# High halves of the second product by ScalarE, earlier writes of plain weight quarters, raw tokens in token buffers

## The chip, the core and the metric

The kernel runs as one program on one core of a Trainium2 chip. The metric is the device time of one execution in microseconds. TensorE does the matmuls (PE in the profile; PEld is its weight load), VectorE is DVE, ScalarE ACT, GpSimd POOL, and SyncE (SP) issues the transfers.

## The reference

Windowed attention over 8 batches, 8 heads, 576 positions and head size 64, and then a feed-forward layer over the 4608 tokens of 512 numbers:

```python
mask_plain = (rel >= 0) & (rel < window)                                    # window 32, heads 0 to 3
mask_dil = (rel >= 0) & (rel < window * dilation) & (rel % dilation == 0)   # dilation 4, heads 4 to 7
attn = softmax(where(mask, q @ k.T / 8, -1e9)) @ v      # (8, 8, 576, 64), then (4608, 512)
h = x @ w_in                                            # (4608, 2048)
g = h * clip(h + 3, 0, 6) / 6
out = g @ w_out                                         # (4608, 512)
```

## The kernel before

**Precision.** Every operand x of a large matmul is held as a high half (a cast to fp32r) and a low half (x minus the high half), and a product is three matmuls: high by high, low by high, high by low.

**Tokens** go in blocks (chunks) of CH = 384. Blocks 0 to 3 are multiplied plainly: first() makes the 12 matmuls of `gemm1` for one of 16 slices f of the hidden layer (L529 to L531), the gate, its high half (L544) and its low half (L548), and second() makes the 9 matmuls of `gemm2` (L579 to L581). Blocks 4 to 11 form four groups g of two blocks, and each 2 by 2 product of blocks is made with seven products in place of eight (Strassen and Winograd's scheme): A11, A12, S2, S1, S3, A22, S4.

**First product of a group** (`first_product`, `multiply`, L732 to L734): for each of eight pairs k of slices seven products of six matmuls; the token operands, `cell(i)`, are filled by `fill` (L700 combines raw tokens on VectorE, L703 casts the high half on ScalarE, L707 subtracts the low half on VectorE). The gate of a result is L982 (ScalarE) and L987 (VectorE). **Second product** (`second_products`): 56 halves, for each a high half gh (L1173), a low half gl (L1179) and six matmuls (L723), with sums of gated tiles between (L1144, VectorE). Its results are taken from the banks by ScalarE (L1096, L1125) and VectorE (L1111). HIGH_BY names the engine of each gh: all "p", GpSimd.

**Weights.** `combine` makes sums of the weights' quarters (words L624, sums L632, high L636, low L641) and `combo_out` (L659) writes them to two tensors in HBM, sums and rights. `combo_plain` (L650) writes the plain quarters there, 24 transfers of 256 KB for each side, after a slice pair's last use in blocks 0 to 3. `load_sums` (L673) brings the tiles back, 512 KB each, into a ring of eight.

**Attention** goes through 48 trios. After the first twelve, `attend` issues a block of scores and values (L213, L231), the exponentials, the turning of tiles, and a load of kq (L184) and v (L193) for the trio two further on. In `low` GpSimd subtracts low halves (L436) for blocks 0 to 3, or copies the tokens of blocks 4 to 11 to raw tiles (L438), from the pool wpool (36 slots, tag w). xh and xl hold the high and low halves of three blocks.

**Order.** ORDER, written by hand, sets the instructions of about the first 75 us. From there each operation is entered with `op(engine, us, do, after, lag, takes, gives, ahead)`: a cost, what it waits for, the buffers that it takes and gives, and how far ahead of its due time it may go. `_in_time` then walks all engines in time and picks, on each, what can start first, and among those what is due first. TensorE's order is fixed; the others' follow from the costs. SyncE's transfers are entered as its issue time with a fixed lag until they land. Every engine runs its queue in order.

Of the kernel before, what the change touches and what calls it, by code (L numbers as in the profile page):

```python
# [19 lines left out]
P = 128  # L20
QB = 32
DIL = 4
# [16 lines left out]
SLACK = 0.4  # L39
SPOTS = (35, 1), (38, 1), (41, 1), (44, 1), (47, 1), (50, 1), (53, 1), (56, 1)  # L40
LEAD_SUMS = 300.0
# [42 lines left out]
def windowed_attention_ffn(ctx: ExitStack, tc: tile.TileContext, qk, vp, w, mask, out, out_t):  # L84
# [87 lines left out]
    def w_tile(name, shape, dtype=F32):  # L172
        return wpool.tile([P, *shape], dtype, name=name, tag="w")
# [211 lines left out]
    def raw_of(block, kind):  # L385

        if (block, kind) not in raws:
            raws[block, kind] = w_tile("raw", [2, CH])
        return raws[block, kind]

    def spans(t):

        b, kind, part = trios[t]
        half = CH // 2
        at = half * part
        while at < half * (part + 1):
            c, i0 = divmod(at, CLS) if kind else (0, at)
            n = min((CLS if kind else S) - i0, half * (part + 1) - at)
            token = b * S + (DIL * i0 if kind else i0)
            if b >= 2:  # L400
                room = CH - token % CH
                n = min(n, room // DIL if kind else room)
            yield at - half * part, n, c, i0, token
            at += n

    def pieces_of(t):

        b, kind, part = trios[t]
        xu = xfs[t].rearrange("p (u f) -> p u f", u=2)
        found = []  # L410
        for at, n, c, i, token in spans(t):
            src, plain = xu[:, :, at : at + n], token < PLAIN * CH
            if plain:
                whole = lambda x: x[:, 2 * kind : 2 * kind + 2, b % 2 * S : b % 2 * S + S]
            else:
                whole = lambda x, token=token: raw_of(token // CH - PLAIN, kind)
                i = token % CH // (DIL if kind else 1)
# [102 lines left out]
    def gemm1(n):  # L520
        c, f = steps[n]
        assert 2 * f in converted and all(x in written for x in trios if c in chunks(*x))
        read[c] += 1
        r0 = (c * CH) % (2 * S)
        ph = ps_h.tile([P, CH], F32, name="ps_h")
        for kt in range(NK):
            a, b = xh[:, kt, r0 : r0 + CH], xl[:, kt, r0 : r0 + CH]
# [3 lines left out]
            ins = nc.tensor.matmul(ph, lhsT=wt(f, 1)[:, ks], rhs=a, start=False, stop=(kt == NK - 1))  # L531
        phs[n] = ph
        return ins
# [140 lines left out]

    seventh = []

    def cell(i):

        if i == S3:
            if not seventh:  # L680
                seventh.extend(w_tile(name, [2, CH], F32R) for name in ("x7h", "x7l"))
            return seventh
        block, k = {A11: (1, 0), A12: (1, 1), S2: (2, 0), S1: (2, 1), A22: (0, 0), S4: (0, 1)}[i]
        return [x[:, 2 * k : 2 * k + 2, block * CH : (block + 1) * CH] for x in (xh, xl)]

# [16 lines left out]
    def fill_high(g, i):  # L702
        nc.scalar.copy(cell(i)[0], source(g, i))  # L703

    def fill_low(g, i):
        hi, lo = cell(i)
        nc.vector.tensor_tensor(out=lo, in0=source(g, i), in1=hi.bitcast(F32), op=ALU.subtract)  # L707
# [18 lines left out]

    def multiply(at, k, i, bank, start):

        tile_, (h, l) = ring[at][:, rows_at(place[k, i] // 2).index(row(k, i))], cell(i)
        for kt in range(2):  # L730
            ks = slice(kt * P, (kt + 1) * P)
            nc.tensor.matmul(bank, lhsT=tile_[:, 0, ks], rhs=h[:, kt], start=(start and kt == 0), stop=False, skip_group_check=True)  # L732
            nc.tensor.matmul(bank, lhsT=tile_[:, 0, ks], rhs=l[:, kt], start=False, stop=False, skip_group_check=True)  # L733
            nc.tensor.matmul(bank, lhsT=tile_[:, 1, ks], rhs=h[:, kt], start=False, stop=(kt == 1), skip_group_check=True)  # L734
# [60 lines left out]
    def attend(bs, pools):  # L795
# [20 lines left out]
        for ts in scores:  # L816
# [15 lines left out]
            if ts + NLOAD < T:  # L832
                landed_k[ts + NLOAD] = op("SP", 0.4, lambda ts=ts: load_qk(ts + NLOAD), [beat], lag=5.0, ahead=EVER)
        for tv in values:
# [11 lines left out]
            if tv + NLOAD < T:  # L846
                landed_v[tv + NLOAD] = op("SP", 0.4, lambda tv=tv: load_v(tv + NLOAD), [beat], lag=5.0, ahead=EVER)
            pieces = [(n, token // CH) for _, n, _, _, token in spans(tv)]
            touched = {c for n, c in pieces if c >= PLAIN} - {c for c, kind in raw_seen if kind == trios[tv][1]}
            raw_seen.update((c, trios[tv][1]) for c in touched)  # L850
# [7 lines left out]
    def put_out(c, tt, bank, r, after, parts, last):  # L858
# [16 lines left out]
        freed.append(done_[-1])  # L875
        op("SP", 0.45, lambda: nc.sync.dma_start(out=out[r : r + P, :], in_=o[0]), done_, lag=2.5, gives=SLOT if last else ())

# [4 lines left out]
    def combine(side, k):  # L882
        x = op("DVE", 0.69, lambda: combo_words(side, k, 0, nc.vector), takes=[("w", 2, 1)], ahead=LEAD_SUMS)
# [46 lines left out]
    def bring(at):  # L930
        if at < 2 * GROUPS * STREAM:
# [3 lines left out]
            elif at < 2 * STREAM:  # L935
                sources = [(1, RIGHT_TURNS[2 * (i - STREAM) + j][1]) for j in range(2)]
            ring_landed[at] = op(
                "SP", 0.5, lambda: load_sums(at), [*(x for y in sources for x in combined[y]), ring_used.get(at - RING)],
                lag=6.0, takes=[("w", 1, 3)], ahead=14.0,
            )  # L940
# [13 lines left out]
    def fill(g, free_after):  # L954
# [42 lines left out]
    def first_product(g, k, i, at_bank, name, after=()):  # L997
# [3 lines left out]
        def do():  # L1001
            if start:
                at_bank[name] = ps_a.tile([P, DM], F32, name="ps_x", tag="ps_a")
            multiply(at, k, i, at_bank[name][:, :CH], start)

# [5 lines left out]
        ring_step(at, x)  # L1011
        used[i] = x
        return x

# [70 lines left out]
    def second_products(g):  # L1085
# [46 lines left out]
        def ship(name, after):  # L1132
# [4 lines left out]

            op("SP", 0.45, do, after, lag=2.5, gives=SLOT)

# [379 lines left out]
```

## Time and profile before

| what | us |
|---|---|
| three runs | 866.81, 871.83 (median), 874.95 |
| the profiled execution | 866.8 |
| its span, first to last instruction | 865.0 |
| TensorE, weight loads busy | 837.4, 774.1 |
| VectorE, ScalarE, GpSimd busy | 699.1, 477.8, 225.6 |
| mean granted clock | 0.992 |
| transfers | 214.71 MB, 248 GB/s on average |

Matmuls are pipelined: one of 384 columns lasts about 335 ns, and the next starts about half of that later. So the sum of durations is no measure of TensorE's work; distances between starts are. The groups of matmuls by stage: `gemm1` and `gemm2` with the attention of the first trios up to about 330 us, then first and second products of the four groups in turn. The second products lie at about 415 to 488, 549 to 618, 678 to 746 and 799 to 861 us.

### The profile page before, as it was taken

What the parts mean: (1) busy time and instruction counts of PE and PEld (TensorE: products, weight loads), DVE (VectorE), ACT (ScalarE), POOL (GpSimd) and SP (SyncE); (2) the same over time, 40 slices, a digit from 0 to 9 for tenths busy, and PEclk for the clock granted to TensorE, in tenths of its full rate; (3) what the DMA queues carried; (4) which work ended last, traced back from release to release, by engine and by line L of the source; (5) the groups of instructions that cost most, each with busy time, mean ns of one, the idle gap of its engine ahead of it and who ended that gap; (6) DMA issues with size and microseconds to landing.
All of it is one profiled execution on the core that took longest, in us unless ns stands there. A gap on an engine that the chain in (4) does not pass through costs nothing.

```text
span 865.0 us, 22224 instructions
## 1 busy us (share of the span) xinstructions
PE 837.4 (97%) x8758; PEld 774.1 (89%) x8758; DVE 699.1 (81%) x1307; ACT 477.8 (55%) x1170; POOL 225.6 (26%) x338
## 2 busy tenths in 40 slices
PE   7899999999999999988999999999999999999998
PEld 4698898988888898977888999998999998999998
DVE  4899986567767988966999977999876899545995
ACT  3788675235999875876801599501598401354100
POOL 0000000010132220000858001558001458001574
PEclk8999999999999999998999999999999999999999
DMA  8856435235338799999974998974988773996371
GB/s 293 278 168 198 125 120 170 86 134 167 127 124 298 254 351 386 380 392 394 366 248 152 315 333 305 339 260 155 328 301 311 266 246 140 356 378 219 131 279 56
DMA packets 115768, 214.71 MB, mean 248 GB/s; under 512 B 7504, under 2 KB 40272, under 8 KB 115664
## 3 DMA queue, kind: packets, MB, share of 16 engines
q1 hardware_dynamic: 115664, 213.29, 71.2%
q8 instruction: 69, 1.13, 0.5%
q14 instruction: 35, 0.29, 0.1%
HBM read 174.47 MB, written 38.80 MB: 247 GB/s over the span
## 4 chain that ended last, share of the span: by engine, by line
PE 78%; DVE 10%; issue 5%; DMA 4%; ACT 2%; POOL 1%; SPq 0%; DVEq 0%; POOLq 0%
PE ps_o L723 15%; PE ps_x L732 8%; PE ps_x L733 8%; PE ps_x L734 8%; DVE gl L1179 6%; PE ps_h L529 5%; PE ps_h L530 5%; PE ps_h L531 5%; PE ps_o L579 5%; PE ps_o L581 5%; PE ps_o L580 5%; DVE g L1144 2%; DMA v<-in_v 2%; PE ps_b L231 2%; PE ps_a L213 1%
## 5 line engine op out<-in xcount | busy, mean ns | idle before, releaser
L723 PE MATMUL ps_o<-gh,ring 128*128 128x384 f32 x896 | 231.9, 335 | 0.1
L1173 POOL CAST gh<-g 128x384 fp32r<-128x384 f32 x224 | 170.5, 793 | 131.8 <-DVE g L987 61.4
L723 PEld LDWEIGHTS ps_o<-gh,ring 128*128 128x128 f32 x896 | 162.4, 188 | 0.8 <-POOL gh L1173 0.4
L723 PE MATMUL ps_o<-gl,ring 128*128 128x384 f32 x448 | 154.2, 344 | 5.8 <-DVE gl L1179 4.7
L1179 DVE TENSOR_TENSOR gl<-g,gh 128x384 fp32r<-128x384 f32 x224 | 152.5, 719 | 1.0 <-POOL gh L1173 1.0
L732 PE MATMUL ps_x<-xh,ring 128*128 128x384 f32 x384 | 132.3, 345 | 2.7 <-DMA ring<-sums 2.7
L733 PE MATMUL ps_x<-xl,ring 128*128 128x384 f32 x384 | 129.9, 338 | 0.0
L734 PE MATMUL ps_x<-xh,ring 128*128 128x384 f32 x384 | 129.6, 338 | 0.0
L723 PEld LDWEIGHTS ps_o<-gl,ring 128*128 128x128 f32 x448 | 84.0, 188 | 17.8 <-DVE gl L1179 17.1
L544 POOL CAST gh<-t 128x384 fp32r<-128x384 f32 x36 | 23.5, 654 | 276.1 <-DVE t L540 276.1
L529 PE MATMUL ps_h<-xh,wi 128*128 128x384 f32 x256 | 87.8, 343 | 0.0
L531 PE MATMUL ps_h<-xh,wi 128*128 128x384 f32 x256 | 86.1, 336 | 0.0
L530 PE MATMUL ps_h<-xl,wi 128*128 128x384 f32 x256 | 86.1, 336 | 0.0
L438 POOL COPY raw<-xf 128x96 f32<-128x96 f32 (+2 forms) x65 | 27.6, 493 | 206.2 <-ACT xf L377 164.2
L1096 ACT ACTIVATE o<-ps_o 128x384 f32<-128x384 f32 x32 | 15.7, 492 | 114.5 <-PE ps_o L723 105.9
L732 PEld LDWEIGHTS ps_x<-xh,ring 128*128 128x128 f32 x384 | 72.6, 189 | 5.9 <-DMA ring<-sums 2.9
L1144 DVE TENSOR_TENSOR g<-g 128x768 f32<-128x768 f32 x64 | 75.2, 1175 | 0.0
L579 PE MATMUL ps_o<-wo,gh 128*128 128x512 f32 x192 | 75.1, 391 | 0.0
L581 PE MATMUL ps_o<-wo,gl 128*128 128x512 f32 x192 | 74.7, 389 | 0.0
L580 PE MATMUL ps_o<-wo,gh 128*128 128x512 f32 x192 | 74.7, 389 | 0.0
L733 PEld LDWEIGHTS ps_x<-xl,ring 128*128 128x128 f32 x384 | 72.6, 189 | 0.2
L734 PEld LDWEIGHTS ps_x<-xh,ring 128*128 128x128 f32 x384 | 72.6, 189 | 0.0
(114 smaller groups left out, 1649.5 us busy)
## 6 DMA issues: line engine op xcount, KB each, us to landing
ring<-sums SPq DMA_DIRECT2D x112, 512.0 KB, 7.5
ring<-rights SPq DMA_DIRECT2D x112, 512.0 KB, 6.4
st<-in_w SPq DMA_DIRECT2D x32, 512.0 KB, 4.2
kq<-in_qk SPq DMA_DIRECT2D x39, 416.0 KB, 4.3
v<-in_v SPq DMA_DIRECT2D x39, 390.0 KB, 5.6
sums<-wi SPq DMA_DIRECT2D x24, 256.0 KB, 6.7
rights<-wo SPq DMA_DIRECT2D x24, 256.0 KB, 6.6
out<-o SPq DMA_DIRECT2D x16, 384.0 KB, 2.8
```

The source lines that it names most:

```text
L529: nc.tensor.matmul(ph, lhsT=wt(f, 0)[:, ks], rhs=a, start=(kt == 0), stop=False)
L530: nc.tensor.matmul(ph, lhsT=wt(f, 0)[:, ks], rhs=b, start=False, stop=False)
L531: ins = nc.tensor.matmul(ph, lhsT=wt(f, 1)[:, ks], rhs=a, start=False, stop=(kt == NK - 1))
L579: nc.tensor.matmul(po[c][tt], lhsT=gh[:, rows], rhs=wt(f, 2), start=first, stop=False)
L580: nc.tensor.matmul(po[c][tt], lhsT=gh[:, rows], rhs=wt(f, 3), start=False, stop=False)
L581: return nc.tensor.matmul(po[c][tt], lhsT=gl[:, rows], rhs=wt(f, 2), start=False, stop=(f == NF - 1))
L723: nc.tensor.matmul(banks[part][:, :CH], lhsT=right[:, a, cols], rhs=x, start=(start and not i), stop=(i == 2), skip_group_check=True)
L732: nc.tensor.matmul(bank, lhsT=tile_[:, 0, ks], rhs=h[:, kt], start=(start and kt == 0), stop=False, skip_group_check=True)
L733: nc.tensor.matmul(bank, lhsT=tile_[:, 0, ks], rhs=l[:, kt], start=False, stop=False, skip_group_check=True)
L734: nc.tensor.matmul(bank, lhsT=tile_[:, 1, ks], rhs=h[:, kt], start=False, stop=(kt == 1), skip_group_check=True)
L1173: nc.gpsimd.tensor_copy(out=two[0], in_=gated_tile(g, q, k))
L1179: nc.vector.tensor_tensor(out=two[1], in0=gated_tile(g, q, k), in1=two[0].bitcast(F32), op=ALU.subtract)
```

## The change

- HIGH_BY becomes all "a": all 224 high halves gh of the second products are copies by ScalarE.
- xh and xl are no longer one tensor each but twelve tiles (three blocks, two kinds of heads, high and low), so each can be given to another use. The raw tokens of the first group (blocks 4 and 5) take the tiles of block 1 when its last matmul is done, in place of four slots of wpool. `spans` now cuts at borders of blocks in all batches.
- `cell(g, i)`: A11, A12 and S3 have tiles of their own; for the first group their fills are ordered S3, A11, S2, S1, A22, S4, A12.
- A transfer is entered as two operations: SyncE's issue, and a stay of `size * 1.3` us on an engine "DMA" of the plan, where one stands behind the other, with a lag of 2.6 us.
- `combo_plain` is entered with no wait, 100 us ahead of its due time at most. The slots of the weights are still given back after the last use.

```diff
-HIGH_BY = ("pppppppp",) * 7
+HIGH_BY = ("aaaaaaaa",) * 7
+LANDING = 2.6
+EARLY = 100.0
...
-    xh = const.tile([P, NK, 2 * S], F32R, name="xh")
-    xl = const.tile([P, NK, 2 * S], F32R, name="xl")
+    def tokens_tile(block, kind, part, name, dtype=F32R):
+        return const.tile([P, 2, CH], dtype, name=name, tag=f"x{block}{kind}{int(part)}")
+    xh, xl = ([[tokens_tile(block, kind, part, f"x{block}") for kind in range(2)] for block in range(3)] for part in (1, 0))
...
-            raws[block, kind] = w_tile("raw", [2, CH])
+            if block < 2:
+                raws[block, kind] = tokens_tile(1, kind, (xl, xh)[block] is xh, "raw", F32)
+            else:
+                raws[block, kind] = w_tile("raw", [2, CH])
...
-            if b >= 2:
-                room = CH - token % CH
-                n = min(n, room // DIL if kind else room)
+            room = CH - token % CH
+            n = min(n, room // DIL if kind else room)
...
+    def transfer(us, size, do, after=(), takes=(), gives=(), ahead=EVER):
+        x = op("SP", us, do, after, takes=takes, ahead=ahead)
+        return op("DMA", size * 1.3, lambda: None, [x], lag=LANDING, gives=gives, ahead=EVER)
...
-        combined[side, k] = [op("SP", 0.9, lambda: combo_out(side, k), [x], lag=3.5, gives=[("w", 2)], ahead=EVER)]
+        combined[side, k] = [
+            transfer(0.9, 2.0, lambda: combo_out(side, k), [x], gives=[("w", 2)]),
+            transfer(1.35, 1.5, lambda: combo_plain(side, k), ahead=EARLY),
+        ]
...
-            combined[side, k].append(
-                op(
-                    "SP", 1.35, lambda: combo_plain(side, k), [words[side, k], taken[side, f - 1], x],
-                    lag=3.5, gives=[("w", 2)], ahead=EVER,
-                )
-            )
+            op("NONE", 0.0, lambda: None, [words[side, k], combined[side, k][1], taken[side, f - 1], x], gives=[("w", 2)], ahead=EVER)
...
-        for i in range(PRODUCTS):
-            x = op("ACT", 0.85, lambda i=i: fill_high(g, i), source[i] + [free_after[i]], takes=[("w", 2)] if g == 0 and i == S3 else ())
-            filled[g, i] = op("DVE", 1.1, lambda i=i: fill_low(g, i), [x, *after[i]], gives=SLOT)
+        order = (S3, A11, S2, S1, A22, S4, A12) if g == 0 else range(PRODUCTS)
+        for i in order:
+            before_high = [filled.get((0, S3)), *([filled[0, A11], filled[0, S4]] if i == A12 else ()), t1, t2, t3, t4] if g == 0 and i in (A11, A12) else ()
+            x = op("ACT", 0.85, lambda i=i: fill_high(g, i), [*source[i], free_after[i], *before_high], takes=[("w", {S3: 2, A11: 1}[i])] if g == 0 and i in (S3, A11) else ())
+            filled[g, i] = op("DVE", 1.1, lambda i=i: fill_low(g, i), [x, *after[i]], gives=() if g == 0 and i in (A11, A12, S3, S4) else SLOT)
```

The rest of the diff enters the loads of kq, v and ring and the writes of results as transfers in the same way, and gives g to `cell` and `multiply`.

The new plan moves instructions at many places; three are shown. Lines are of each kernel's own file.

**SyncE where the first ring loads begin.** Before (L650 writes plain quarters, L659 combined weights, L673 loads the ring):

```order
L650 DMA rights<-wo 256x1x256 x3
L650 DMA sums<-wi 256x1x256 x3
L659 DMA sums<-sh 128x4x256
L659 DMA sums<-v 128x4x256
L650 DMA rights<-wo 256x1x256 x3
L673 DMA ring<-sums 128x2x512 x2
L650 DMA sums<-wi 256x1x256 x3
L673 DMA ring<-sums 128x2x512 x3
L650 DMA sums<-wi 256x1x256 x3
L673 DMA ring<-sums 128x2x512 x2
```

Now (L657, L666 and L680 are the same three):

```order
L666 DMA sums<-sh 128x4x256
L666 DMA sums<-v 128x4x256
L657 DMA rights<-wo 256x1x256 x15
L190 DMA kq<-in_qk 128x832
L199 DMA v<-in_v 128x780
L190 DMA kq<-in_qk 128x832
L199 DMA v<-in_v 128x780
L680 DMA ring<-sums 128x2x512 x7
L666 DMA rights<-sh 128x4x256
L666 DMA rights<-v 128x4x256
```

No plain quarter stands among or behind the ring loads any more; the combined right weights still stand among them.

**The second product of the second group, ScalarE.** Before (L703 fills tokens, L1125 and L1096 take banks; the 48 casts L1173 stand in GpSimd's queue):

```order
L703 CAST xh<-raw 128x2x384
L982 ACTIVATE t<-s,three 128x384
L1125 COPY ps_o<-ps_o 128x384 x2
L703 CAST xh<-raw 128x2x384 x2
L1096 ACTIVATE o<-ps_o 128x384 x6
L703 CAST xh<-t 128x2x384 x3
L703 CAST x7h<-raw 128x768
```

Now (L716, L1145 and L1116 are those three, L1195 is the cast of gh):

```order
L716 CAST cell<-raw 128x768
L1195 CAST gh<-g 128x384 x4
L1000 ACTIVATE t<-s,three 128x384
L716 CAST cell<-raw 128x768
L1195 CAST gh<-g 128x384
L1145 COPY ps_o<-ps_o 128x384 x2
L1195 CAST gh<-g 128x384 x6
L716 CAST x_79<-raw 128x768
L1195 CAST gh<-g 128x384 x4
L1116 ACTIVATE o<-ps_o 128x384 x2
```

The casts of gh now stand between the fills and the evictions of ScalarE's one queue.

**ScalarE at the start of the first group.** Before (L537 is the Relu of block 3, L636 the weights' cast):

```order
L703 CAST x7h<-raw 128x768
L293 ACTIVATE x<-ps_a,z 128x64 x2
L537 ACTIVATE t<-ps_h,three 128x384
L636 CAST sh<-v 128x1024
L537 ACTIVATE t<-ps_h,three 128x384
L377 COPY a<-a_t 32x192 x4
L537 ACTIVATE t<-ps_h,three 128x384 x2
L703 CAST xh<-t 128x2x384
L703 CAST xh<-raw 128x2x384
L1053 COPY ps_x<-ps_x 128x384
```

Now:

```order
L643 CAST sh<-v 128x1024
L544 ACTIVATE t<-ps_h,three 128x384 x2
L716 CAST x_79<-raw 128x768
L544 ACTIVATE t<-ps_h,three 128x384
L716 CAST x_78<-t 128x768
L643 CAST sh<-v 128x1024
L716 CAST cell<-raw 128x768
L1073 COPY ps_x<-ps_x 128x384
```

x_79 and x_78 are S4 and A22; the last cast is A12's, which before was made among the earlier fills.

More of the change, by code (lines that the diff above doesn't have):

```diff
@@ L673, in load_sums, with cell @@
         nc.sync.dma_start(out=ring[at].bitcast(F32).rearrange("p n a x -> p n (a x)"), in_=rows.rearrange("n p a x -> p n (a x)"))
[L675 to L684, printed above, removed]
+    cells = {}
+    def cell(g, i):
+        if i in (A11, A12, S3):
+            x = (i, min(g, 1)) if i == A11 else (i, 0)
+            if x not in cells:
+                second_place = lambda part, kind: tokens_tile(1, kind, part, "cell")
+                small = lambda: w_tile("cell", [2, CH], F32R)
+                cells[x] = {
+                    (A11, 0): lambda: [second_place(1, 0), small()], (A12, 0): lambda: [second_place(0, 0), second_place(1, 1)],
+                    (A11, 1): lambda: [cells[A11, 0][0], second_place(0, 1)], (S3, 0): lambda: [small(), small()],
+                }[x]()
+            return cells[x]
+        block, kind = {S2: (2, 0), S1: (2, 1), A22: (0, 0), S4: (0, 1)}[i]
+        return [x[block][kind] for x in (xh, xl)]
     sources = {}
@@ L725, in multiply_right, with multiply @@
                 )
-    def multiply(at, k, i, bank, start):
-        tile_, (h, l) = ring[at][:, rows_at(place[k, i] // 2).index(row(k, i))], cell(i)
+    def multiply(at, g, k, i, bank, start):
+        tile_, (h, l) = ring[at][:, rows_at(place[k, i] // 2).index(row(k, i))], cell(g, i)
         for kt in range(2):
@@ L846, in attend @@
             if tv + NLOAD < T:
-                landed_v[tv + NLOAD] = op("SP", 0.4, lambda tv=tv: load_v(tv + NLOAD), [beat], lag=5.0, ahead=EVER)
+                landed_v[tv + NLOAD] = transfer(0.4, 0.77, lambda tv=tv: load_v(tv + NLOAD), [beat])
             pieces = [(n, token // CH) for _, n, _, _, token in spans(tv)]
-            touched = {c for n, c in pieces if c >= PLAIN} - {c for c, kind in raw_seen if kind == trios[tv][1]}
+            x = [*x, ends_of[1]] if any(PLAIN <= c < PLAIN + 2 for n, c in pieces) else x
+            touched = {c for n, c in pieces if c >= PLAIN + 2} - {c for c, kind in raw_seen if kind == trios[tv][1]}
             raw_seen.update((c, trios[tv][1]) for c in touched)
@@ L875, in put_out @@
         freed.append(done_[-1])
-        op("SP", 0.45, lambda: nc.sync.dma_start(out=out[r : r + P, :], in_=o[0]), done_, lag=2.5, gives=SLOT if last else ())
+        transfer(0.45, 0.5, lambda: nc.sync.dma_start(out=out[r : r + P, :], in_=o[0]), done_, gives=SLOT if last else ())
     gated_h = {}
@@ L882, in combine @@
     def combine(side, k):
-        x = op("DVE", 0.69, lambda: combo_words(side, k, 0, nc.vector), takes=[("w", 2, 1)], ahead=LEAD_SUMS)
+        x = op("DVE", 0.69, lambda: combo_words(side, k, 0, nc.vector), takes=[("w", 2, SPARE[side][k])], ahead=LEAD_SUMS)
         words[side, k] = x = op("DVE", 0.69, lambda: combo_words(side, k, 1, nc.vector), [x], ahead=EVER)
@@ L936, in bring @@
                 sources = [(1, RIGHT_TURNS[2 * (i - STREAM) + j][1]) for j in range(2)]
-            ring_landed[at] = op(
-                "SP", 0.5, lambda: load_sums(at), [*(x for y in sources for x in combined[y]), ring_used.get(at - RING)],
-                lag=6.0, takes=[("w", 1, 3)], ahead=14.0,
+            ring_landed[at] = transfer(
+                0.5, 1.0, lambda: load_sums(at), [*(x for y in sources for x in combined[y]), ring_used.get(at - RING)],
+                takes=[("w", 1, 3)], ahead=14.0,
             )
@@ L1003, in do @@
                 at_bank[name] = ps_a.tile([P, DM], F32, name="ps_x", tag="ps_a")
-            multiply(at, k, i, at_bank[name][:, :CH], start)
+            multiply(at, g, k, i, at_bank[name][:, :CH], start)
         x = op(
@@ L1012, in first_product @@
         used[i] = x
+        if (g, i, k) == (0, A11, PAIRS - 1):
+            plan[x].gives.append(*SLOT)
         return x
```

16 lines of the change are left out of this document (8 added, 8 removed).

## The prediction

> **What bounds the kernel now.** I read the page first: busy shares, chain, groups. Then the waits of TensorE and of its weight loads, the stages that hold them, and the instructions of the named lines one by one.
>
> ```profile
> PE 837.4 (97%) x8758; PEld 774.1 (89%) x8758; DVE 699.1 (81%) x1307; ACT 477.8 (55%) x1170; POOL 225.6 (26%) x338
> PE 78%; DVE 10%; issue 5%; DMA 4%; ACT 2%; POOL 1%; SPq 0%; DVEq 0%; POOLq 0%
> PEld ps_o L723 <- DVE gl L1179: 17.1, 36, 0.8
> PE ps_b L231 <- DMA v<-in_v: 5.0, 3, 3.4
> PE ps_x L732 <- DMA ring<-sums: 2.7, 3, 1.5
> ```
>
> The first row is busy time by engine, the second the shares of the chain that ended last; the others are waits (total us, times, longest). TensorE bounds the kernel and can lose only its holes. Two kinds matter: 36 short waits of the second product's weight loads for the low halves (gl, L1179), 17.1 us, and six waits for transfers, 7.7 us. What the first 60 us lose is not touched on purpose.
>
> The holes of the first kind sit where VectorE never rests:
>
> ```profile
> 574.00:600.00 26.00, 24.80 (x133) 22.50 (x132) 26.00 (x32) 3.15 (x6) 21.11 (x26) 1.00 0.76 270
> 555.33 18.74 PE ps_o L723 x108
> L1179 DVE TENSOR_TENSOR gl<-g,gh 128x384 fp32r<-128x384 f32 x22 | 16.4, 782 | 0.0
> L1144 DVE TENSOR_TENSOR g<-g 128x768 f32<-128x768 f32 x7 | 8.8, 1252 | 0.0
> L1173 POOL CAST gh<-g 128x384 fp32r<-128x384 f32 x26 | 22.1, 890 | 4.9 <-DVE g L1144 1.9 <-PE ps_o L723 1.7 <-DVE gl L1179 1.3
> ```
>
> The first row is one stretch of the second group's second product (busy PE, PEld, DVE, ACT, POOL, then clock, DMA share, GB/s): VectorE 26.00 of 26 us, GpSimd 21.11 beside it, ScalarE 3.15. The second row is an undisturbed run of matmuls, 18.74/108 = 0.1735 us each; the stretch's 133 need 23.1 us, so 2.9 of its 26 are lost. The other rows are that stretch's groups. Now what those instructions take at other times:
>
> ```profile
> L1179 DVE TENSOR_TENSOR gl<-g,gh x224: 509/850/891, 415.1 to 854.9; 128x384 fp32r<-128x384 f32 x112
> L1144 DVE TENSOR_TENSOR g<-g x64: 941/1252/1275, 417.0 to 840.2; 128x768 f32<-128x768 f32 x64
> L1173 POOL CAST gh<-g x224: 499/826/1244, 413.8 to 852.2; 128x384 fp32r<-128x384 f32 x112
> L1173 POOL CAST gh<-g 128x384 fp32r<-128x384 f32 x224 | 170.5, 793 | 131.8 <-DVE g L987 61.4
> L548 DVE TENSOR_TENSOR gl<-t,gh 128x384 fp32r<-128x384 f32 x64 | 35.5, 555 | 9.0 <-POOL gh L544 8.4 <-ACT gh L544 0.6
> L544 ACT CAST gh<-t x28: 495/513/527, 44.2 to 154.8; 128x384 fp32r<-128x384 f32 x28
> ```
>
> (Min/median/max in ns.) The low half runs 509 at best and 850 at the median; the same subtraction earlier, L548, with high copies by ScalarE or a mostly idle GpSimd, has a mean of 555. The sums L1144 run 941 or 1252. GpSimd's copy swings alike, 499 to 826 at the median. These two engines slow each other by about 0.3 us whenever both work.
>
> The second kind of hole belongs to one saturated stretch:
>
> ```profile
> 300.00:415.00 115.00, 107.24 (x1440) 98.13 (x1428) 92.25 (x198) 83.11 (x219) 12.45 (x21) 0.97 1.04 374
> 200.00:300.00 100.00, 100.00 (x1618) 87.67 (x1618) 73.21 (x178) 83.90 (x275) 22.39 (x42) 1.00 0.60 199
> 375.00:400.00 25.00, 19.38 (x279) 17.56 (x278) 15.96 (x41) 17.41 (x48) 1.01 (x2) 0.89 1.07 394
> 400.00:425.00 25.00, 23.83 (x216) 22.08 (x216) 21.36 (x43) 21.63 (x58) 12.22 (x26) 0.97 1.05 389
> ```
>
> From 300 to 415 us the DMA engines are full (share 1.04) at 374 GB/s; before that they are at 0.60. The clock reads 0.89 and 0.97 after the worst wait: 25 x 0.11 + 25 x 0.03 = 3.5 us at most, part of it while TensorE stood anyway. I count 2.3, so this kind costs 10 (7.7 to 11.2).
>
> **The change part by part.**
>
> *High copies to ScalarE.* All 224 casts of L1173 go from GpSimd, where they took 170.5 us, to ScalarE at 0.513 (L544): 115 us more, 593 in all of some 850. In the stretch above that is 26 x 0.513 = 13.3 on 3.15 of 26 us, so it hides behind the matmuls, and VectorE loses its neighbour. The stretch's VectorE work becomes 22 x 0.555 + 10 x 0.945 (seven sums, three wide token operations) = 21.7 us instead of 26, against 23.1 of matmuls: 1.4 us of room where 2.9 were short. Of the 17.1 us I keep 2 (0 to 7), for the start of each group and places where a low half follows two sums: gain 15.1. If ScalarE's cover fails, the price is in the rivals.
>
> *Quarters written sooner, transfers in the plan.* The 48 plain quarter writes no longer wait for the words or last uses. In the order before, 30 of them stand behind the last two pairs of kq and v ahead of the ring loads, which go out at about 300 us; now none does, all stand ahead. That is 30 x 0.262 = 7.9 MB out of 115 x 374 = 43.0 MB. These rows give their size and the rate of a full queue:
>
> ```profile
> rights<-wo SPq DMA_DIRECT2D x18, 256.0 KB, 6.7
> sums<-wi SPq DMA_DIRECT2D x12, 256.0 KB, 7.2
> GB/s 111 334 342 372 363 288 348 400 398 400 383 382 381 380 384 385 391 387 385 370 362 392 383 395 386 383 395 392 401 384 394 405 398 396 387 392 385 388 396 388
> ```
>
> (Window 300 to 420 us; the last row is 40 slices of it.) At 388 GB/s the stretch's 43.0 MB take 111 us, while TensorE without the 10 us of stalls needs 105: the queue ends last. 35.1 MB take 90: TensorE does. The writes land in 200 to 300 us, where 19.9 MB become 27.8, 278 GB/s, below what the queue carries. The ring loads, kq and v keep their order, and all eight combined right weights (two transfers of 0.524 MB each) still stand among the first ring loads, so a crowded spot stays. I keep 2 of the 10 (0 to 6): gain 8.
>
> The Trainium skill (DMA: Bandwidth & Descriptors, Where 436 GB/s comes from) puts a core's share of HBM at about 358 GB/s; the slices above show 380 to 405, so here the trace decides. By the page's figure 35.1 MB would take 98 us, still under 105, and I would keep about 4 instead of 2.
>
> *Raw tokens in token buffers, tokens cut by block.* The copies to raw stay on GpSimd, in other tiles. Trios of the first two batches are now cut at block borders, six pieces more on VectorE and on ScalarE. What a piece costs:
>
> ```profile
> L436 DVE TENSOR_TENSOR xl<-xf,xh 128x288 fp32r<-128x288 f32 x4 | 2.8, 702 | 0.0
> L436 DVE TENSOR_TENSOR xl<-xf,xh 128x192 fp32r<-128x192 f32 x4 | 1.9, 512 | 0.0
> L436 DVE TENSOR_TENSOR xl<-xf,xh 128x96 fp32r<-128x96 f32 x4 | 1.3, 334 | 0.0
> L430 ACT CAST xh<-xf 128x288 fp32r<-128x288 f32 x4 | 2.9, 733 | 0.0
> 24.77 0.97 DVE xl L436 x2
> 29.10 0.85 DVE xl L436 x2
> ```
>
> Splitting 288 into 192 and 96 adds 512 + 334 - 702 = 144 ns; six on each engine are 0.9, and some 1.3 on ScalarE. The last two rows are pieces of the chain, so a part goes straight onto the path. I take 0.7 (0.3 to 2.2).
>
> *Order of the first group's fills.* A12's high and low halves now come last, behind S4 and A22, which wait for the last matmuls of the fourth chunk. From there ScalarE has three casts, a Relu and a weights' cast in line, then VectorE a subtraction; their rows:
>
> ```profile
> L703 ACT CAST xh<-raw 128x768 fp32r<-128x768 f32 x12 | 9.8, 842 | 0.0
> L636 ACT CAST sh<-v 128x1024 fp32r<-128x1024 f32 x16 | 16.7, 1051 | 3.7 <-DVE v L632 3.6
> L537 ACT ACTIVATE t<-ps_h,three 128x384 f32<-128x384 f32 x64 | 37.0, 582 | 51.3 <-PE ps_h L531 50.9
> L707 DVE TENSOR_TENSOR x7l<-raw,x7h 128x768 fp32r<-128x768 f32 x4 | 3.8, 946 | 0.0
> ```
>
> 3 x 0.842 + 0.582 + 1.051 + 0.946 = 5.1 us. TensorE has meanwhile A11 and S2 (12 matmuls), 18 wider matmuls of the last chunk and an attention block before it needs A12: over 30 x 0.1735 = 5.2 us. That is close, so I take 0.5 (0 to 2.5, were the weights' words late for their cast). Free slots of wpool cost nothing.
>
> **Sum.** The profiled execution took 866.8 us (span 865.0): 866.8 - 15.1 - 8 + 0.7 + 0.5 = 844.9. The runs' median, 871.83, is 5.0 above it. I can't tell from one trace what made the slower runs; transfers at the limit are likely, and those go. I add 1.1: **846 us**. The best end of all terms is 866.8 - 17.1 - 11.2 + 0.3 = 838.8, the worst 866.8 - 10.1 - 4 + 2.2 + 2.5 = 857.4.
>
> **The rivals.**
>
> *The transfers bind all the same.* The eight combined right weights, 16 x 0.524 = 8.4 MB, stay beside ring, kq and v, and stalls of 10 us just move there. For it: every slice was at 380 or more. Against it: 90 of 105 us. Then 866.8 - 15.1 + 1.2 = 853.
>
> *VectorE stays slow.* If the 0.3 us came from the matmuls' reads and not from GpSimd, the low halves stay at 850 and nothing of the 17.1 comes back: 866.8 - 8 + 1.2 = 860. Against it: L548 ran at 555 beside matmuls.
>
> *Copies queue behind evictions, slower.* A copy on ScalarE stands in line with the evictions that wait for TensorE:
>
> ```profile
> ACT o L1096 <- PE ps_o L723: 105.9, 13, 24.6
> L1096 ACT ACTIVATE o<-ps_o 128x384 f32<-128x384 f32 x32 | 15.7, 492 | 114.5 <-PE ps_o L723 105.9
> ```
>
> At an end of a product two evictions, then copy and low half, come to 2 x 0.492 + 0.513 + 0.555 = 2.05 us from TensorE's last matmul to its next operand, unless earlier pairs are stocked. Seven ends in four groups at half that price are 29 us: 866.8 - 21.9 + 29 = 874. It decides from about 0.8 us an end. Against it: in the new order copies for several steps stand ahead of each pair of evictions, and TensorE takes 6 x 0.1735 = 1.04 us over each step.
>
> *Nothing changes* (the two gains eaten by waits that I don't see): 866.
>
> **Chances.** Forecast 0.74, transfers bind 0.11, VectorE stays slow 0.06, queue behind evictions 0.05, nothing 0.04. A measurement of this kernel can tell about 1% from no change. 846 and 853 are faster by more; 860 is at the border and I halve it; with nothing, same. Faster 0.88, same 0.07, slower 0.05. Range 837 to 861: the terms' ends, opened at the top to the second rival.
>
> The Trainium skill (TensorE: Matmul & The Clock Gate, HAM oscillation) says that idle gaps of over about 3.4 us throttle the clock. The trace agrees: the longest wait above was 3.4, and 0.89 follows. By that rule the clock's share of the second gain is all or nothing, 3.5 or 0.
>
> **What would show it.** Right: in the second products gl at a mean of 0.55 to 0.57 and the sums near 0.95; the weight loads' wait for gl under 5 us; VectorE not full in any such stretch; GpSimd near 55 us busy, ScalarE near 590; DMA share below 1 in part of 300 to 400 us, TensorE's waits for v and ring under 4 us in all, clock 1.00 there. Wrong: gl still at 0.7; waits for ring or v of 8 us or more; weight loads that wait for gh by ScalarE; a first 60 us longer by over 2.

## The result, and the profile after

The changed kernel takes 843.64 us (median of four runs, 842.75 to 846.16), the kernel before 869.39 (four runs, 866.81 to 874.95): a ratio of 0.970, 95% interval 0.964 to 0.976. The forecast was 846, with a range of 837 to 861. The profiled execution of the changed kernel took 846.16 us (span 844.0), the slowest of its four, while that of before, 866.8, was the fastest of its four.

Busy time, the shares of the chain that ended last, and what the weight loads of the second product still wait for:

```profile
PE 828.2 (98%) x8758; PEld 776.8 (92%) x8758; DVE 646.7 (77%) x1313; ACT 573.7 (68%) x1400; POOL 55.5 (7%) x114
PE 96%; ACT 2%; issue 1%; DVE 1%; DMA 0%; SPq 0%; DVEq 0%
PEld ps_o L736 <- DVE gl L1199: 0.9, 2, 0.5
PEld ps_o L736 <- ACT gh L1195: 0.8, 1, 0.8
```

VectorE lost 52 us of busy time although it got six instructions more. The wait for the low halves is 0.9 us where it was 17.1, the chain's share of VectorE 1% where it was 10%. Only one weight load waits for a copy by ScalarE.

The instructions of the second products by line (min/median/max in ns), and a stretch of the second group's second product by engine:

```profile
L1199 DVE TENSOR_TENSOR gl<-g,gh x224: 542/550/709, 409.9 to 833.6; 128x384 fp32r<-128x384 f32 x112
L1164 DVE TENSOR_TENSOR g<-g x64: 942/950/1106, 411.3 to 817.0; 128x768 f32<-128x768 f32 x64
L1195 ACT CAST gh<-g x224: 496/514/540, 409.2 to 831.0; 128x384 fp32r<-128x384 f32 x112
564.00:590.00 26.00, 26.00 (x152) 26.00 (x151) 23.15 (x40) 15.91 (x33) 0.00 (x0) 1.00 0.80 286
```

Medians of 550 and 950 ns where 850 and 1252 stood, VectorE at 23.15 of 26 us where it was full, GpSimd at nothing.

The stretch of the transfers (engines, then clock, DMA share, GB/s), and the plain right quarters' writes between 300 and 415 us; the first row is of the kernel before, for the last 65 us of the stretch, the others of the changed kernel:

```profile
350.00:415.00 65.00, 57.24 (x843) 52.99 (x842) 48.15 (x112) 49.65 (x127) 4.73 (x12) 0.95 1.06 389
300.00:415.00 115.00, 114.24 (x1506) 104.58 (x1505) 99.67 (x215) 93.59 (x247) 15.11 (x26) 1.00 1.00 362
350.00:415.00 65.00, 64.24 (x894) 60.26 (x893) 55.37 (x131) 58.72 (x155) 7.67 (x16) 1.00 1.05 387
375.00:400.00 25.00, 25.00 (x410) 23.86 (x410) 21.90 (x56) 23.14 (x65) 1.87 (x3) 1.00 1.06 393
rights<-wo SPq DMA_DIRECT2D x15, 256.0 KB, 4.8
```

TensorE is busy through 375 to 400 us, with no wait for v or ring anywhere and the clock at 1.00, though the DMA engines are as full there (1.06, 393 GB/s) as before.

Both kernels run the same 8758 matmuls in one order, so the start of each in one trace can be set against its start in the other. The offset (after minus before) of a matmul that starts, in the trace of before, at:

| at (us) | 30 | 40 | 360 | 410 | 480 | 610 | 740 | 860 |
|---|---|---|---|---|---|---|---|---|
| offset (us) | +1.1 | +4.4 | +4.5 | -5.9 | -12.0 | -15.5 | -19.3 | -21.1 |

So the first 40 us lost 4.4, the transfers gave 10.4 back between 360 and 410, and the second products 6.1, 3.5, 3.8 and 1.8, 15.2 together.

### The profile page after: what moved, and what is told of

Its sections match the earlier page's. It is cut to its first block, busy times and chain, and to the rows that moved or that the text cites. A ratio compares the mean times of both kernels' runs of the same rounds, so it can differ in the third digit from the quotient of the medians.

```text
span 844.0 us, 22143 instructions
## 1 busy us (share of the span) xinstructions
PE 828.2 (98%) x8758; PEld 776.8 (92%) x8758; DVE 646.7 (77%) x1313; ACT 573.7 (68%) x1400; POOL 55.5 (7%) x114
## 4 chain that ended last, share of the span: by engine, by line
PE 96%; ACT 2%; issue 1%; DVE 1%; DMA 0%; SPq 0%; DVEq 0%
PE ps_o L736 28%; PE ps_x L745 9%; PE ps_x L747 9%; PE ps_x L746 9%; PE ps_h L536 6%; PE ps_h L537 5%; PE ps_h L538 5%; PE ps_o L586 5%; PE ps_o L588 5%; PE ps_o L587 5%; PE ps_b L237 2%; PE ps_a L219 1%; PE ps_a L229 1%; PE ps_b L219 1%; PE ps_a L237 1%; PE ps_a L345 1%
## 5 line engine op out<-in xcount | busy, mean ns | idle before, releaser
L736 PE MATMUL ps_o<-gl,ring 128*128 128x384 f32 x448 | 149.9, 335 | 0.3 <-DVE gl L1199 0.2
L1199 DVE TENSOR_TENSOR gl<-g,gh 128x384 fp32r<-128x384 f32 x224 | 116.5, 553 | 28.2 <-ACT gh L1195 26.0
L1195 ACT CAST gh<-g 128x384 fp32r<-128x384 f32 x224 | 104.3, 513 | 27.8 <-PE ps_o L736 20.3
L745 PE MATMUL ps_x<-x,ring 128*128 128x384 f32 x256 | 88.5, 346 | 0.0
L536 PE MATMUL ps_h<-x,wi 128*128 128x384 f32 x256 | 88.3, 345 | 0.0
L537 PE MATMUL ps_h<-x,wi 128*128 128x384 f32 x256 | 86.4, 338 | 0.0
L538 PE MATMUL ps_h<-x,wi 128*128 128x384 f32 x256 | 86.4, 337 | 0.0
L746 PE MATMUL ps_x<-x,ring 128*128 128x384 f32 x256 | 86.2, 337 | 0.0
L747 PE MATMUL ps_x<-x,ring 128*128 128x384 f32 x256 | 86.1, 336 | 0.0
L586 PE MATMUL ps_o<-wo,gh 128*128 128x512 f32 x192 | 75.1, 391 | 0.0
L544 ACT ACTIVATE t<-ps_h,three 128x384 f32<-128x384 f32 x64 | 37.0, 582 | 49.8 <-PE ps_h L538 49.0
L747 PE MATMUL ps_x<-cell,ring 128*128 128x384 f32 x192 | 64.8, 338 | 0.0
L746 PE MATMUL ps_x<-cell,ring 128*128 128x384 f32 x192 | 64.7, 337 | 0.0
L745 PE MATMUL ps_x<-cell,ring 128*128 128x384 f32 x192 | 64.7, 337 | 0.0
L1164 DVE TENSOR_TENSOR g<-g 128x768 f32<-128x768 f32 x64 | 60.8, 952 | 0.0
L547 DVE SCALAR_TENSOR_TENSOR t<-t,ps_h 128x384 f32<-128x384 f32 x64 | 35.0, 548 | 29.1 <-ACT t L544 28.7
L1049 DVE TENSOR_TENSOR s<-ps_x,s 128x384 f32<-128x384 f32 x64 | 35.2, 550 | 24.5 <-ACT s L1042 20.4
```

The source lines that it names most:

```text
L586: nc.tensor.matmul(po[c][tt], lhsT=gh[:, rows], rhs=wt(f, 2), start=first, stop=False)
L736: nc.tensor.matmul(banks[part][:, :CH], lhsT=right[:, a, cols], rhs=x, start=(start and not i), stop=(i == 2), skip_group_check=True)
L1195: nc.scalar.copy(two[0], gated_tile(g, q, k))
L1199: nc.vector.tensor_tensor(out=two[1], in0=gated_tile(g, q, k), in1=two[0].bitcast(F32), op=ALU.subtract)
```

## The experiments

**High copies back on GpSimd.**

```diff
-HIGH_BY = ("aaaaaaaa",) * 7
+HIGH_BY = ("pppppppp",) * 7
```

> The changed kernel with the 224 high copies of the second products given back to GpSimd; the rest of the change stays. Theory (VectorE and GpSimd slow each other): the low halves go back to a mean of about 0.78 us, the weight loads wait for them again some 14 to 17 us, the time is 843.6 + 15 = 859 (856 to 862). Rival (the new plan, which knows more of the transfers, set the copies and low halves in a better order, and the engine matters little): low halves slow or not, waits stay under 6 us and the time is 844 to 849.

856.66 us (855.61 to 860.06). Its low halves and its weight loads' wait:

```profile
L1199 DVE TENSOR_TENSOR gl<-g,gh x224: 510/850/891, 404.2 to 844.7; 128x384 fp32r<-128x384 f32 x112
PEld ps_o L736 <- DVE gl L1199: 16.8, 37, 0.7
```

The slow low halves and the whole wait return, with the new plan in place. 13.0 us of the change belong to the copies' engine; the rival falls.

**The copies by ScalarE alone, on the kernel before.**

```diff
-HIGH_BY = ("pppppppp",) * 7
+HIGH_BY = ("aaaaaaaa",) * 7
```

> The kernel before with nothing changed but the engine of the 224 high copies, ScalarE. Theory: low halves at 0.55 us, their waits under 2 us, 869.4 - 15 = 854 (851 to 857), and the stalls for v and ring of 350 to 425 us stay at 8 to 11 us. Rival (the gains need each other, since the first group's second product starts late behind the stalled transfers, or ScalarE needs the new plan): 858 to 869.

855.36 us (852.39 to 856.61), 13.9 less than the 869.26 of the kernel before beside it.

```profile
L1179 DVE TENSOR_TENSOR gl<-g,gh x224: 545/552/711, 416.5 to 842.6; 128x384 fp32r<-128x384 f32 x112
PE ps_b L231 <- DMA v<-in_v: 6.1, 3, 3.8
PE ps_x L732 <- DMA ring<-sums: 1.8, 3, 0.8
```

The low halves are fast, and the waits for v and ring stay as they were (6.1 and 1.8 us). The copies need nothing else of the change.

**Plain quarters late again, in the changed kernel.**

```diff
         combined[side, k] = [
             transfer(0.9, 2.0, lambda: combo_out(side, k), [x], gives=[("w", 2)]),
-            transfer(1.35, 1.5, lambda: combo_plain(side, k), ahead=EARLY),
         ]
...
-            op("NONE", 0.0, lambda: None, [words[side, k], combined[side, k][1], taken[side, f - 1], x], gives=[("w", 2)], ahead=EVER)
+            combined[side, k].append(
+                transfer(1.35, 1.5, lambda: combo_plain(side, k), [words[side, k], taken[side, f - 1], x], gives=[("w", 2)])
+            )
```

> The changed kernel with the plain quarters written after the words and last uses again, transfers still entered in the plan with their sizes. Theory (the late quarters, 30 x 0.262 MB beside the ring loads, are what made the transfers late): TensorE waits for v and ring again, 6 to 11 us, 843.6 + 9 = 853 (849 to 856). Rival (the plan's knowledge of transfers is what orders kq, v and ring in time): waits under 3 us, 843 to 847.

850.24 us (848.26 to 852.89), 6.6 over the changed kernel, less than the 9 expected.

```profile
PE ps_x L745 <- DMA ring<-sums: 4.9, 2, 4.7
350.00:415.00 65.00, 59.96 (x858) 55.56 (x857) 49.80 (x115) 52.26 (x138) 3.93 (x10) 0.95 1.05 386
```

The stall is back, in another place: a ring load, not v, comes 4.7 us late, and the clock reads 0.95. But 855.36 (copies alone) against 850.24 here says that the rest of the change, with transfers entered in the plan, is worth about 5 us as long as the quarters are late. Which part of that rest it is, no run separates.

**Early quarters alone, on the kernel before.**

```diff
         combined[side, k] = [
             op("SP", 0.9, lambda: combo_out(side, k), [x], lag=3.5, gives=[("w", 2)], ahead=EVER),
+            op("SP", 1.35, lambda: combo_plain(side, k), lag=3.5, ahead=100.0),
         ]
...
-            combined[side, k].append(
-                op(
-                    "SP", 1.35, lambda: combo_plain(side, k), [words[side, k], taken[side, f - 1], x],
-                    lag=3.5, gives=[("w", 2)], ahead=EVER,
-                )
-            )
+            op("NONE", 0.0, lambda: None, [words[side, k], combined[side, k][1], taken[side, f - 1], x], gives=[("w", 2)], ahead=EVER)
```

> The kernel before with the plain quarters entered with no wait, and nothing else: transfers are still entered as an issue with a fixed lag, copies stay on GpSimd. Theory: the waits for v and ring fall from 7.7 to under 3 us, 869.4 - 9 = 860 (857 to 863), low halves stay slow. Rival (it is the plan's knowledge of transfers): 866 to 870.

855.61 us (855.37 to 858.39), 13.7 less than before, more than the 9 expected. Between the two traces 10.5 of it lie from 360 to 410 us and 0.8 at the start; the other 2.4 come from the basis, since the traced execution of before lies that far under the median of its runs. In its trace no matmul waits for v or ring (one weight load waits 0.3 us for a ring tile), and it keeps the wait for the low halves:

```profile
350.00:415.00 65.00, 63.63 (x890) 59.60 (x889) 56.86 (x125) 59.05 (x153) 14.30 (x29) 1.00 1.06 391
PEld ps_o L723 <- DVE gl L1177: 16.9, 39, 0.7
```

So the early writes remove the stall without the plan's knowledge of transfers. Where the writes stood is seen in SyncE's queue of the kernel before (start, length of the issue, transfers) and then of the changed one:

```profile
337.01 0.85 SPq L193 DMA_DIRECT2D v<-in_v  x1
337.90 2.02 SPq L650 DMA_DIRECT2D rights<-wo  x3
...
340.87 2.94 SPq L650 DMA_DIRECT2D rights<-wo  x3
...
348.27 2.60 SPq L650 DMA_DIRECT2D rights<-wo  x3
351.77 0.35 SPq L184 DMA_DIRECT2D kq<-in_qk  x1
...
353.01 2.39 SPq L650 DMA_DIRECT2D rights<-wo  x3
355.56 0.50 SPq L673 DMA_DIRECT2D ring<-sums  x1
```

```profile
300.18 14.56 SPq L657 DMA_DIRECT2D rights<-wo  x15
314.84 0.56 SPq L190 DMA_DIRECT2D kq<-in_qk  x1
...
316.90 4.39 SPq L680 DMA_DIRECT2D ring<-sums  x7
...
330.82 0.85 SPq L680 DMA_DIRECT2D ring<-sums  x1
339.81 0.34 SPq L190 DMA_DIRECT2D kq<-in_qk  x1
```

Before, twelve writes of 256 KB stand between ring, kq and v from 338 to 355 us, 3.1 MB or 8 us at 388 GB/s, ahead of the stall. After, the last fifteen are out by 315, and the queue pauses before 340: the kq load there waits 8.1 us for its buffer, not for a place.

**GpSimd copies aside, in the changed kernel.** Three copies for each high copy, from the mask to a tile that nobody reads.

```diff
+    aside = const.tile([P, P], F32R, name="aside")
...
-                    nc.scalar.copy(two[0], gated_tile(g, q, k))
+                    behind = nc.scalar.copy(two[0], gated_tile(g, q, k))
+                    for _ in range(3):
+                        beside = nc.gpsimd.tensor_copy(out=aside, in_=mi.bitcast(F32)[:, P : 2 * P])
+                        tc.add_manual_dep(
+                            beside.ins, behind.ins.name, mybir.DependencyInfo(mybir.DependencyClass.Sync, mybir.DependencyReason.DATA), reason="beside"
+                        )
```

> The changed kernel, and beside every high copy by ScalarE three copies of 128x128 words on GpSimd from the mask to a tile that nobody reads: no result and no wait of another engine hangs on them. Theory (the two engines slow each other when both use SBUF, whoever waits for whom): low halves near 0.75 to 0.85 us, weight loads wait for them 12 us or more, 843.6 + 13 = 857 (852 to 861). Rival (low halves were late because they waited for GpSimd's copies, not because they were slow): low halves at 0.55, 843 to 846.

873.08 us (869.54 to 875.03): more than either side expected, and not for the reason meant.

```profile
L1199 POOL CAST aside<-mi 128x128 fp32r<-128x128 f32 x672 | 304.7, 453 | 78.1 <-ACT gh L1197 36.0
L1206 DVE TENSOR_TENSOR gl<-g,gh 128x384 fp32r<-128x384 f32 x224 | 132.4, 627 | 8.6 <-ACT gh L1197 8.3
PEld ps_o L738 <- DVE gl L1206: 1.1, 2, 0.6
PE ps_x L747 <- ACT s L1044: 10.6, 2, 8.2
ACT t L1002 <- POOL raw L448: 10.0, 1, 10.0
850.00:871.00 21.00, 2.10 (x13) 1.77 (x11) 0.00 (x0) 0.98 (x2) 17.09 (x59) 0.66 0.05 19
```

The low halves slowed to 627 only, and TensorE hardly waits for them. The copies took GpSimd 304.7 us, so its own work came late: a copy of raw tokens in its queue held ScalarE up for 10.0 us and TensorE behind it (10.6), and the last row shows it working alone after the last matmuls. Beside the changed kernel's second trace the matmuls lose 14.7 us and the end another 15.6. As a test of the slow low halves it is inconclusive: the forecast of 0.75 to 0.85 us for them failed too. The wide copies below were made for that.

**GpSimd memsets aside.** As above, with the copy replaced:

```diff
-                        beside = nc.gpsimd.tensor_copy(out=aside, in_=mi.bitcast(F32)[:, P : 2 * P])
+                        beside = nc.gpsimd.memset(aside.bitcast(F32), 0.0)
```

> As the run with three GpSimd copies aside, but with memsets of 128x128 words, which write SBUF and read nothing. Theory A (any traffic of GpSimd slows VectorE): low halves 0.7 us or more, 852 to 858. Theory B (it is the reading of two operands on both sides that collides, as only VectorE's instructions with both inputs in SBUF slowed in the trace of before): low halves at 0.55, 843 to 847. I lean to B.

841.78 us (840.85 to 843.29).

```profile
L1199 POOL MEMSET aside<- x672: 204/205/262, 405.5 to 827.8; 128x128 f32 x168
L1206 DVE TENSOR_TENSOR gl<-g,gh x224: 546/554/656, 405.6 to 828.9; 128x384 fp32r<-128x384 f32 x112
```

672 GpSimd instructions that only write SBUF, in the same places, leave the low halves at 554 ns, where copies of the same size brought them to a mean of 627. So it is GpSimd's reading that slows them. That VectorE's side of theory B holds too, an instruction with one operand from SBUF not being slowed, is seen in the run with wide copies below.

**Both parts without the rest.** The kernel before with the copies' line and the early quarters' edit shown above.

> The kernel before with the copies by ScalarE and the early quarters, nothing else: no block cuts, no raw tokens in token buffers, no new order of the first group's fills, no transfers in the plan. If the two parts add up: 869.3 - 13.9 - 13.7 = 841.7 (840 to 844). If the cut pieces at the start cost the changed kernel 1 to 3 us, this is faster than the changed kernel on the same chip by that; if the rest of the change is needed for the transfers or for the copies, it is slower, 846 to 852.

843.87 us (841.88 to 844.48); and **the changed kernel beside it**, with nothing edited:

> The changed kernel itself on the same chip as the others of this call, as their measure: 843.6 (842 to 846). Its trace gives a second draw of the first 60 us: if the cut pieces cost time there, the granted clock is under 0.7 at 30 to 35 us again and the first 75 us lose 21 us or more; if it was chance, they lose 19 to 20 and the clock is 1.00 as in the kernel before.

843.49 us (841.25 to 843.61). The two can't be told apart: the two parts carry the whole result, and neither the cut pieces nor the new order of fills shows in the time. The sum of the parts, 841.7, was 2 us too hopeful. In this second trace of the changed kernel the matmuls of the first 40 us start 3.0 us earlier than in the first, with the same program, the clock is 1.00 from 30 to 40 us, and one ring load comes late, by 0.6 us.

**One slot less, as a control,** and **wide copies aside.** The tile of the wide copies needs room:

```diff
-SLOTS_W = 36
+SLOTS_W = 35
```

> The changed kernel with 35 instead of 36 slots of wpool, to make room for the next run's tile: its control, since the plan shifts a little. 843.5 (842 to 847), low halves at 0.556.

844.76 us (843.29 to 848.22). Then, on top of it:

```diff
+    aside = const.tile([P, CH], F32R, name="aside")
...
-                    nc.scalar.copy(two[0], gated_tile(g, q, k))
+                    behind = nc.scalar.copy(two[0], gated_tile(g, q, k))
+                    beside = nc.gpsimd.tensor_copy(out=aside, in_=mi.bitcast(F32)[:, P : P + CH])
+                    tc.add_manual_dep(
+                        beside.ins, behind.ins.name, mybir.DependencyInfo(mybir.DependencyClass.Sync, mybir.DependencyReason.DATA), reason="beside"
+                    )
```

> As the control with 35 slots, and beside each of ScalarE's 224 high copies one copy of 128x384 words on GpSimd from the mask to a tile that nobody reads: the size and number that GpSimd had in the kernel before, half of the load of the run with three small copies, and again no one waits for it. Theory (the engines slow each other by the share of time in which both move SBUF operands): low halves back at a median near 0.85 us, sums near 1.25, weight loads wait for the low halves 12 to 18 us, 15 us over the control. Rival (in the kernel before the low halves were late for waiting on GpSimd's copies): low halves slow, but waits under 5 us and at most 4 us over the control.

859.63 us (855.62 to 861.69), 14.9 over the control.

```profile
L1198 POOL CAST aside<-mi x224: 509/730/1269, 406.4 to 847.3; 128x384 fp32r<-128x384 f32 x112
L1205 DVE TENSOR_TENSOR gl<-g,gh x224: 540/852/859, 406.4 to 849.2; 128x384 fp32r<-128x384 f32 x112
L1166 DVE TENSOR_TENSOR g<-g x64: 943/1253/1262, 411.5 to 835.2; 128x768 f32<-128x768 f32 x64
L1133 DVE SCALAR_TENSOR_TENSOR o<-ps_o,o x16: 511/544/547, 467.4 to 847.8; 128x384 f32<-128x384 f32 x16
PEld ps_o L738 <- DVE gl L1205: 15.7, 35, 1.6
```

Nobody waits for the copies aside, and everything of the kernel before is back: 852 and 1253 ns, and 35 waits with 15.7 us. The low halves were late because they were slow, and they were slow because GpSimd read SBUF beside them. The fourth row is VectorE's eviction, which takes one operand from a bank and one from SBUF: 10 of its 16 run beside a copy for most of their length, and all stay at 511 to 547 ns. The low halves and the sums, which are slowed, take both operands from SBUF.

**Every second copy by GpSimd.**

```diff
-HIGH_BY = ("aaaaaaaa",) * 7
+HIGH_BY = ("apapapap",) * 7
```

> The changed kernel with every second high copy on GpSimd. If the cost goes with the number of copies on GpSimd, half of the 13 us between all on ScalarE and all on GpSimd: 850 (848 to 853). If it is a threshold, VectorE's sums in a step going beyond TensorE's time only with all copies on GpSimd (21.7 + 11 x 0.3 = 25.0 us of VectorE in a stretch where TensorE needs 23.1, against 26 and over with all), it is between the two too, near 852; if half of the load still fits under the matmuls, 844 to 846.

841.36 us (839.98 to 843.29), no slower than with all copies by ScalarE, and below all three forecasts; the nearest is the third, that half of the load still fits under the matmuls. The first row is of the kernel before, for comparison:

```profile
549.00:618.00 69.00, 67.74 (x466) 64.54 (x465) 68.90 (x97) 15.35 (x28) 41.18 (x50) 1.00 0.72 241
L1199 DVE TENSOR_TENSOR gl<-g,gh 128x384 fp32r<-128x384 f32 x224 | 139.3, 659 | 2.7 <-POOL gh L1193 1.6 <-ACT gh L1195 0.9
PEld ps_o L736 <- DVE gl L1199: 1.2, 2, 0.8
550.00:610.00 60.00, 60.00 (x524) 59.31 (x523) 54.77 (x91) 27.66 (x63) 13.26 (x20) 1.00 0.74 262
```

A low half takes 659 ns in the mean, VectorE as a whole 24 us more than with none (670.8 against 646.7 us), and TensorE waits 1.2 us. Over the second group's second product VectorE is busy 54.77 of 60 us, where it was 68.90 of 69: it now ends before TensorE. The run with three small copies agrees: VectorE is at 670.8 us there too, and TensorE waits 1.1 us for the low halves. So the cost is a threshold, not a price per copy. My estimate of 25.0 us against 23.1 came from one stretch of 26 us. That the sum over the product counts instead, because copies and low halves are made some steps ahead, is my reading; no run tests it.

## Why the prediction was right, point by point

- **Low halves: right, in mechanism and size.** 15.1 us forecast, 15.2 between the traces; 13.0 and 13.9 by the runs with this part undone and alone. The wide copies aside show the cause itself, with nobody waiting on GpSimd. The rival of matmul reads as the cause is out: with the copies alone moved to ScalarE, the matmuls are the same and the low halves run at 552 ns. The Trainium skill (SBUF — State Buffer, Who interferes with whom) says that a VectorE instruction with two SBUF inputs contends with a GpSimd instruction that reads SBUF, and not with one that only writes it. The runs agree with both halves: a median of 852 ns beside wide copies and 639 beside small ones, 554 beside memsets of the small size.
- **Copies on ScalarE: hidden, as forecast.** 513 ns each, one wait of 0.8 us; the rival of queueing behind evictions did not happen.
- **Transfers: right in place, too small in size, and the working of the step failed.** 8 us forecast, 10.4 between the traces, 13.7 by the medians with this part alone. I argued by volume: all thirty writes, 7.9 MB, out of the stretch, so that the queue would end before TensorE. In fact fifteen of them still fall behind 300 us, the stretch carries 115 x 362 = 41.6 MB where it was 43.0, and from 350 us on the DMA engines are as full as ever (387 against 389 GB/s). By my own reckoning 41.6 MB at 388 GB/s, 107 us, would still have bound TensorE at 105. Three ring loads more, 1.6 MB, are among them, since the kernel is further on by 415 us; without them it would be 103, so the volume is too near the limit to decide anything. "Every slice was at 380 or more", in the first rival, was misread too: 9 of the 40 slices lie at 111 to 372. What changed is which transfers stand ahead: no plain write stands among ring, kq and v after 315 us, and SyncE's queue has caught up before 340. The sign "DMA share below 1 in part of 300 to 400 us" came there (0.86 from 325 to 350, where it was 1.07). Whether the order itself or this lead makes the later loads early enough, no run separates. Nor did the eight combined right weights, for which I kept 2 us, cost any in this trace.
- **Pieces at the start: forecast 0.7, the traces show 4.4, the runs show nothing sure.** By its own sign (first 60 us longer by over 2) this step was wrong in that execution. Two rows of the kernel before, then three of the changed one, the last of them pauses of TensorE in which it waits for nothing that the profile shows:

```profile
30.00:35.00 5.00, 3.68 (x184) 2.75 (x185) 4.76 (x13) 2.86 (x7) 0.00 (x0) 1.00 0.97 319
35.00:40.00 5.00, 4.30 (x59) 3.94 (x45) 4.34 (x10) 3.54 (x8) 0.00 (x0) 1.00 1.03 406
30.00:35.00 5.00, 4.00 (x121) 3.04 (x122) 3.71 (x9) 3.49 (x9) 0.00 (x0) 0.68 0.96 320
35.00:40.00 5.00, 3.64 (x116) 2.72 (x105) 2.63 (x9) 0.00 (x0) 0.00 (x0) 0.50 0.99 372
PE ps_a L219 <- issue: 3.8, 3, 1.5
```

  Before, both stretches ran at a clock of 1.00. Take the matmul that starts at 75.1 us in the trace of before. In the four traces without the cuts it starts at 74.4 to 76.5 us (mean 75.3), in the nine with them at 74.8 to 79.6 (mean 77.3). The nine lie 4.8 us apart, two traces of the very same kernel 3.1, more than the means differ. So 3.1 of the 4.4 us were this execution's and not the program's. Executions differ in when the clock is at 0.50. Three traces have it there in the same two stretches of the first 75 us (10.0 to 13.5 and 20.2 to 23.7): the changed kernel's second, the copies alone and the early quarters alone. From 25 to 75 us, where all cut pieces lie, the changed kernel falls 0.4 us behind the one and 1.1 behind the other, which fits the 0.7 forecast; these are single traces. One thing stays open: a fall of the clock to 0.50 that begins between 30.8 and 32.9 us is in eight of the nine traces with the cuts and in none of the four without. The program may favour it.

  The prediction quoted the Trainium skill's rule on idle gaps of over about 3.4 us (TensorE: Matmul & The Clock Gate, HAM oscillation). In the changed kernel's first trace the clock fell to 0.50 from 32 to 42 us with no gap between matmuls over 1.5 us in the 24 us ahead of it, though the gaps of these 24 us add up to 5.9. In the trace of before, which the prediction called in agreement, the clock fell at 394.5 us, when the wait of 3.4 us had lasted for 0.9. The measurement decides: neither fall had such a gap ahead of it.
- **Order of the first group's fills: 0.5 forecast, 0.1 between the traces.** The 5.1 us line ended in time.
- **The level.** 844.9 for the sum and 846.16 for the profiled execution: errors of -2.4 (transfers), -0.4 (fills) and +3.7 (start) nearly cancelled, which is luck. The 1.1 us added for the median had the wrong sign: here the median lies 2.5 below the profiled execution. That this one lost its time at the start is likely, since the second trace, at 843.49 us, did not lose it; the other three executions have no trace. What made the slower runs of before stays open.

## What to carry to other kernels

Before work is put on GpSimd "for free", look at what VectorE does beside it: the same instruction at two durations, each steady, is the sign, and the price falls due only once VectorE's sum passes the time of the engine that bounds the kernel, so moving half of the work can give all of the gain. Where one queue issues all transfers, read which of them stand ahead of the late one, not how full the DMA engines are: from 350 us on they were as full after as before, and nobody waited. And of a trace's first microseconds take a second draw before a difference there is believed.

## What the runs showed of the hardware that was not expected

- One GpSimd copy of 128x384 costs a VectorE instruction with two SBUF inputs 0.31 us, however long that is (medians in the kernel before without a copy beside and with one: 546 and 852 ns, 945 and 1252). The copy itself goes from 509 ns at best to 730 in the median in the run with wide copies. ScalarE's casts stay at means of 511 to 514 in all these runs, and a VectorE instruction with one operand from a bank at 511 to 547 beside the wide copies. Three copies of 128x128, which keep GpSimd busy longer (304.7 against 187.9 us), cost a low half only some 0.09 us (a median of 639 ns).
- A DMA share of 1.05 to 1.06 for 65 us, at 387 to 391 GB/s, went with waits of TensorE for v and ring of 0.3 us at most, in the two traces shown with early writes.
